# A 32-head attention with a gated MLP on one core: the first tiles of x and V's weights in another order, and a unit's shift by one-tensor steps

## The chip, the core and the metric

The kernel runs on one core of a Trainium2 chip. The metric is the device time of one execution in microseconds. The kernel before takes 1639.81 us, the median of three runs (1638.86 to 1640.61).

## The reference

x is 2048 x 512, in float32. There are 32 heads of 16 elements; the MLP has 1792 hidden elements.

```python
xn = _layernorm(x, axis=-1)
qkv = (xn @ wqkv).reshape(B, S, 3, H, Dh)            # q, k, v
scores = einsum("bhqd,bhkd->bhqk", q, k) * Dh ** -0.5
s = (softmax(scores) @ v).reshape(B, S, D) @ wo
h = xn @ w1 + b1
g = silu(square(max(h, 0)) @ w2 + b2)
return x + s * g
```

## The kernel before, in words

Every product is made in float32 from three reduced products: each operand is split into a high and a low part, and high x high, high x low and low x high are added up (`terms3`). A split is two instructions, one that rounds to the high part and one that subtracts it (L82 and L83 on GpSimd; with `hi_act` the first is on ScalarE).

**The ramp** (loop at L1146 to L1172) brings 16 tiles of x through the layernorm: statistics on VectorE (`ln_stats`), the normalized tile on ScalarE (`ln_norm`, L1089), four transposes on TensorE and the high part on ScalarE (`ln_high`, L1096 and L1098), the low part on VectorE (`ln_low`, L1104). V's weights (`wa_t`, four pieces of 128 rows called ko 0 to 3) are split on GpSimd ahead of the loop (L1144). Between the transposes, `pump(n)` puts n matmuls of a waiting tile of Q, K or V on TensorE (L991); such a full-array tile has 12 matmuls. Each engine works through its own list in the order in which the program is written.

**The lead loop** (L1212 to L1260) makes the rest of Q, K and V in half-array pieces, 24 matmuls to a tile (`lead_halves`, L1040). Beside them run the first max matmuls (L305) with their reductions (L313): for each query row, the largest score over 512 keys is taken.

**The main loop** has 512 slots. 16 slots make a unit, a quad of heads with a quarter of the queries. A slot has four score matmuls (L1283), four exponentials (L1289), four groups of products with V (L379, here called PV), and between them max matmuls for later units and the matmuls of the MLP (L239, L207) and of the output product (L787), which are called dense work. `long_slots` (L1365) handles two slots at a time in one of two forms. The form of *seven* has seven max matmuls and runs the PV groups of two slots together, 16 matmuls in a row. The form of *eight* has eight max matmuls and two separate runs of 8. Whether a pair of slots takes the form of seven is decided by `ahead_m`: only if enough maxima have been made for the units to come. `hosts` picks the slots in which a unit's shift falls.

**The shift of a unit** (`shift`, L336 to L365) follows the unit's last max reduction by two slots (`late`, L332). It reduces 64 partial maxima to 16 (L338), makes the high and the low part of the negated maximum (L340 and L343, two instructions that read two tensors each; L340 reads a tile of zeros) and transposes them (L347). Then `keep` writes them to HBM (`sh_d`, L350) one slot later, and `back` reads them as two more rows of the score matmul's operand (`qe`, L370). Unit u needs these rows at slot 16u. `later(n, fn)` puts such a step on a waiting list that is worked off n slots later, in the order of the list; the DMAs themselves go through one queue, SyncE's, in that same order. On it stand, near the end, also `wo_small` (L675, four small loads of the tile h, L682), the output product's operand (`oc`, L701), the tiles g and xr of the output (L726, L731), the stores of the finished heads (`on_d`, L426) and the loads of q for the max matmuls (`qm`, L135 and L140).

**The output** of a tile (`post`, L770 to L782) multiplies the product with g on VectorE (L780) and adds x on GpSimd.

Of the kernel before, what the change touches and what calls it, by code (L numbers as in the profile page):

```python
# [8 lines left out]
F32 = mybir.dt.float32  # L9
F32R = mybir.dt.float32r  # L10
# [6 lines left out]
P = 128  # L17
# [23 lines left out]
def kernel(  # L41
# [28 lines left out]
    make_identity(nc, ident)  # L70
    eps_t = const.tile([P, 1], F32, name="eps_t")
    nc.vector.memset(eps_t, EPS)
    zero = const.tile([P, 16], F32, name="zero")
    nc.vector.memset(zero, 0.0)
    b1_t = const.tile([P, FO], F32, name="b1_t")
    b2_t = const.tile([P, D], F32, name="b2_t")

# [20 lines left out]
    with ExitStack() as ph:  # L98
# [84 lines left out]
        waiting = []  # L183
        now = [0]

        def later(n, fn):
            waiting.append((now[0] + n, fn))

        def run_waiting(all_=False):
            due = [w for w in waiting if all_ or w[0] <= now[0]]  # L190
# [138 lines left out]
                if s == 15:  # L329
                    late.append((now[0] + 2, u))  # L330

        def shift_due():  # L332
            if late and late[0][0] <= now[0]:
                shift(late.pop(0)[1])

        def shift(u):  # L336
            m4 = sp.tile([P, 16], F32, name="m4")
            nc.vector.tensor_reduce(m4, mxs[u], axis=AX.X, op=ALU.max)  # L338
            sh = sp.tile([P, 2, 16], F32R, name="sh")
            nc.vector.scalar_tensor_tensor(  # L340
                sh[:, 0], m4, -1.0, zero, op0=ALU.mult, op1=ALU.add
            )
            nc.vector.scalar_tensor_tensor(  # L343
                sh[:, 1], m4, -1.0, sh[:, 0].bitcast(F32), op0=ALU.mult, op1=ALU.subtract
            )
            sq = sp.tile([P, 32], F32, name="sq")
            nc.vector.transpose(sq, sh.rearrange("p i c -> p (i c)").bitcast(F32))  # L347

            def keep():
                nc.sync.dma_start(sh_d[u].rearrange("r (b q) -> b r q", q=32), sq)  # L350

            def back():
                for p in range(2):
                    for i in range(2):
                        shift_rows(u, p, i)

            if in_loop:
                later(1, keep)
                later(max(2, 16 * u - 9 - now[0]), back)
            else:  # L360
                keep()
                if u < 2:
                    back()
                else:
                    waiting.append((16 * u - 9, back))  # L365
# [371 lines left out]
        def wo_part():  # L737
            for k in range(15):
                c, tt = WO_ORDER[k]
                if k == 0:  # L740
                    later(2, lambda: wo_load(3))
                if k == 2:
                    later(2, lambda: wo_load_last(3))
                if k == 5:
                    wo_load(0)
                if k == 6:
                    later(2, lambda: wo_load_last(0))
                if k == 9:
# [12 lines left out]
                g, xr = wos.pop(k)  # L761
                wide = c < 2 and m_free()
                if wide and "w" not in free_ps:
                    free_ps["w"] = [pm.tile([P, 512], F32, name="pm_t") for _ in range(3)]
                ps = [pd.tile([P, D], F32, name="pd_t")]
                ps.append(free_ps["w"][2] if wide else ps[0])
                if c > 1:
                    s = tail[c, tt] = tail["p"].tile([P, D], F32, name=f"ts{c}{tt}")

                def post():  # L770
                    if c > 1:
                        nc.scalar.activation(s, ps[0], AF.Copy)
                        nc.gpsimd.tensor_tensor(s, s, g, op=ALU.mult)
                        nc.gpsimd.tensor_tensor(s, s, xr, op=ALU.add)
                        return
                    if wide:
                        h = wos["f"].tile([P, D], F32, name="h", bufs=2)
                        nc.vector.tensor_tensor(h, ps[1], g, op=ALU.mult)
                        nc.gpsimd.tensor_tensor(xr, xr, h, op=ALU.add)
                    nc.vector.tensor_tensor(g, ps[0], g, op=ALU.mult)  # L780
                    nc.gpsimd.tensor_tensor(g, g, xr, op=ALU.add)
                    later(2, lambda g=g, t0=t0: nc.sync.dma_start(of[t0 : t0 + P, :], g))  # L782

                def emit(lane, n, i, m, kos):
                    r = slice(64 * lane, 64 * lane + 64)
                    a, b = ((0, 0), (0, 1), (1, 0))[i]
                    inst = nc.tensor.matmul(  # L787
                        ps[lane], oc[r, a, n, ts_], wot[r, b, n],
                        start=m == 0 and (lane == 0 or wide), stop=m == kos and (lane == 1 or wide),
                        skip_group_check=True,  # L790
                    )
                    if m == 0 and last_use[0] is not None and not wide:
                        tc.add_manual_dep(
                            inst.ins, last_use[0].ins.name,
                            mybir.DependencyInfo(
                                mybir.DependencyClass.Sync, mybir.DependencyReason.DATA
                            ),
                            reason="the other row tile is done with the bank",
                        )

                units = []
                for lane in range(2):
                    kos = [0, 1, 2] + [3] * (c < 2 or lane == 0)
                    terms = [(n, i) for n in kos for i in range(3)]
# [336 lines left out]
            load_x(t)  # L1141
        for vt in vts:
            nc.vector.memset(vt[:, :, DH:], 1.0)
        for ko in range(KO):  # L1144
            split((wa_t[:, 0, ko, 2 * P :], wa_t[:, 1, ko, 2 * P :]), raw_v[:, ko])
        for i in range(NT + 3):  # L1146
            if i == 1:
                ln_norm(0)
            if i < NT:
                ln_stats(i)  # L1150
            if 0 < i - 1 < NT:
                ln_norm(i - 1)
            if 0 <= i - 3 < NT:
                ln_low(i - 3)
            if 0 <= i - 2 < NT:
                ln_high(i - 2)
            if i in (3, 4):
                kos = slice(2 * i - 6, 2 * i - 4)
                split((wa_t[:, 0, kos, : 2 * P], wa_t[:, 1, kos, : 2 * P]), raw_m[:, kos])
            if 6 <= i < 10:  # L1160
                fill_ring("ka", i // 2 - 3, 1.0, (32 + 64 * (i % 2),))
            if i in (10, 11):
                fill_ring("qm", i - 10, 0.0)
            if i == 11:
                raw_r = [load_w("wv", 3 * P, ((P, 3 * P),))]
            if i >= 3:
                rest.append(("v", (i - 3) % 4, (i - 3) // 4))
                if i % 4 == 2:
                    c = (i - 3) // 4
                    ahead.append(("qk", 4, c))  # L1170
                    (rest if c else ahead).append(("qk", 0, c))
                pump(8 if i > 3 else 6)  # L1172
        while ahead:
            pump(1)
        lx.close()
# [131 lines left out]
        def dense():  # L1307
# [3 lines left out]
            wo_pools()  # L1311
            wo_ask(0)
            wo_ask(1)
            later(3, wo_small)
            yield from wo_part()

        pts = {}
# [37 lines left out]
                n + 4 * max(0, 16 * u - SHIFT - st) >= 64 * (u + 1) for u in range(n // 64, NU)  # L1355
            )

        host = [0]

        def hosts(st):  # L1360
            if late and st > host[0] + 4:
                host[0] = st + 2
            return st <= host[0]

        def long_slots(st0, units, post, wide=False):  # L1365

# [25 lines left out]
            for h in range(2):  # L1392
# [4 lines left out]
                if wide:  # L1397
# [9 lines left out]
                    shift_due()  # L1407
                    for kb in (st - 2, st - 1):
                        pv_step(kb, pts.pop(kb))
                elif n == 12 and ahead_m(  # L1410
                    sum(done_m) + 7 - (0 if hosts(st) else max(0, 450 - st) // 16 * 2), st + 2
                ):
                    visit(h, "s" + "D" * n + "s", ".mmsmssmsmssmm")
                    begin(st + 1)
                    max_end()
# [3 lines left out]
                else:  # L1419
# [2 lines left out]
                    else:  # L1422
                        visit(h, "D" * n + ".", "msmsmsmsms")
                    max_end()
                    shift_due()
                    pv_step(st - 2, pts.pop(st - 2))
                    begin(st + 1)
                    if n == 12:
# [1 line left out]
                    else:  # L1430
                        visit(h, "ss..", "mmsm", True)
                    max_end()
                    shift_due()
                    pv_step(st - 1, pts.pop(st - 1))
            if post is not None:
                last_use[0] = None
# [90 lines left out]
```

## Time and profile before

| | |
|---|---|
| median of three runs | 1639.81 us |
| the profiled execution | 1642.99 us |
| its span in the profile | 1641.1 us |
| TensorE busy | 1621.3 us |
| VectorE busy | 1350.6 us |
| ScalarE busy | 1181.7 us |
| GpSimd busy | 516.4 us |

The span runs from the first to the last instruction in the trace; the profiled execution's own time has 1.9 us more around it, and lies 3.2 us above the median of the runs. Rows of a timeline give the start, the duration, the engine, the line, the operation, what it writes and reads, and in brackets how long its engine had been idle before and what ended that. SPq is SyncE's queue; its rows are DMA issues, not transfers. In the chain of waits, a row gives the start, the duration and the engine of one piece of the chain that ended last.

### The profile page before, as it was taken

How to read it: one execution, taken by the hardware profiler on the slowest of the kernel's cores; microseconds unless marked ns; L12 is line 12 of the kernel's file. 1: busy time of each engine (PE TensorE's matmuls, PEld its weight loads, DVE VectorE, ACT ScalarE, POOL GpSimd, SP SyncE). 2: the span in 40 equal slices, each digit the busy share in tenths (PEclk: the TensorE clock that was granted, in tenths of full speed). 3: DMA queues.
4: the chain of work that ended last, by engine and by line, in shares of the span. 5: the costliest groups of instructions: out<-in, count | busy, mean ns of one | idle time of the engine just before them, and what ended most of it. 6: DMA issues, size and time to landing. Idle time of an engine off the chain costs nothing.

```text
span 1641.1 us, 35386 instructions
## 1 busy us (share of the span) xinstructions
PE 1621.3 (99%) x13627; PEld 979.2 (60%) x13627; DVE 1350.6 (82%) x2335; ACT 1181.7 (72%) x2339; POOL 516.4 (31%) x541
## 2 busy tenths in 40 slices
PE   7999999999999999999999999999999999999998
PEld 6799666556656655565566556645665565454455
DVE  6399988887788888888888888888888888888843
ACT  6221477778878877787777777877877777777785
POOL 5335567513211321222123103311331133213224
PEclk9899999999999999999999999999999999999999
DMA  8596555426232522342333423343341442415444
GB/s 304 158 270 222 180 177 163 130 54 170 86 87 83 162 72 81 102 128 70 93 99 111 114 71 111 95 107 82 112 121 50 105 142 62 105 48 171 122 147 143
DMA packets 150465, 201.44 MB, mean 123 GB/s; under 512 B 50008, under 2 KB 67416, under 8 KB 148760
## 3 DMA queue, kind: packets, MB, share of 16 engines
q1 hardware_dynamic: 150296, 199.17, 41.6%
q8 instruction: 108, 1.77, 0.5%
q14 instruction: 61, 0.50, 0.1%
HBM read 144.84 MB, written 53.99 MB: 121 GB/s over the span
## 4 chain that ended last, share of the span: by engine, by line
PE 94%; DVE 2%; issue 2%; DMA 1%; POOL 0%; SPq 0%; ACT 0%; DVEq 0%
PE po L379 30%; PE pm_t L305 17%; PE pd_t L239 17%; PE se L1283 15%; PE pd_t L207 5%; PE se L1040 3%; PE pd_t L787 2%; DVE mx L313 2%; PE pd_t L1040 1%; PE po L1040 1%; PE se L991 1%; DMA ka<-k_d 1%; PE pm_t L1283 0%; DMA xt<-in_A_x_dram 0%; POOL wr_t L944 0%
## 5 line engine op out<-in xcount | busy, mean ns | idle before, releaser
L313 DVE TENSOR_REDUCE mx<-pm_t 128x1 f32<-128x512 f32 x2048 | 1267.9, 683 | 208.7 <-PE pm_t L305 123.1
L1289 ACT ACTIVATE pt<-se 128x512 f32<-128x512 f32 x1738 | 924.0, 615 | 227.3 <-PE se L1283 156.5
L305 PE MATMUL pm_t<-ka,qm 64*128 64x512 f32 x2048 | 784.5, 418 | 4.2 <-DVE mx L313 2.4
L1283 PE MATMUL se<-qe,ka 64*128 64x512 f32 x2009 | 735.0, 413 | 0.4 <-DMA qe<-sh_d 0.2
L379 PE MATMUL po<-pt,v 128*32 128x512 f32 x3554 | 526.6, 602 | 0.0
L305 PEld LDWEIGHTS pm_t<-ka,qm 64*128 64x128 f32 x2048 | 360.6, 185 | 219.5 <-DVE mx L313 205.2
L1283 PEld LDWEIGHTS se<-qe,ka 64*128 64x128 f32 x2009 | 350.5, 184 | 103.1 <-ACT pt L1289 61.8
L239 PEld LDWEIGHTS pd_t<-xc,w1s 64*128 64x128 f32 x2352 | 295.7, 187 | 47.3 <-issue 45.3
L239 PE MATMUL pd_t<-xc,w1s 64*128 64x256 f32 x2352 | 322.0, 286 | 0.0
L239 PE MATMUL pd_t<-w2t,hT 64*128 64x512 f32 x936 | 253.2, 406 | 0.0
L379 PE MATMUL po<-ex,v 128*32 128x512 f32 x542 | 226.5, 602 | 0.0
L1289 ACT ACTIVATE ex<-se 128x512 f32<-128x512 f32 x271 | 163.4, 616 | 42.1 <-PE se L1283 30.2
L239 PEld LDWEIGHTS pd_t<-w2t,hT 64*128 64x128 f32 x936 | 159.5, 184 | 48.5 <-issue 40.2
L379 PEld LDWEIGHTS po<-pt,v 128*32 128x32 f32 x3554 | 88.2, 108 | 154.3 <-issue 141.1
L558 POOL TENSOR_TENSOR r<-r 128x512 f32<-128x512 f32 x49 | 50.9, 1039 | 331.9 <-ACT r L555 331.9
L577 POOL TENSOR_TENSOR u<-u,b_t 128x512 f32<-128x512 f32 x16 | 20.7, 1296 | 365.0 <-ACT u L576 365.0
L207 PE MATMUL pd_t<-w2t,hT 64*128 64x512 f32 x408 | 106.1, 392 | 0.0
L207 PEld LDWEIGHTS pd_t<-w2t,hT 64*128 64x128 f32 x408 | 72.5, 184 | 9.6 <-DVE mx L313 0.7
L787 PE MATMUL pd_t<-wot,oc 64*128 64x512 f32 x267 | 76.9, 406 | 0.0
L417 POOL TENSOR_TENSOR ot<-ot,hl 128x512 f32<-128x512 f32 x31 | 39.8, 1284 | 109.1 <-DMA hl<-r_d 80.9
L83 POOL TENSOR_TENSOR hT<-r,hT 128x512 fp32r<-128x512 f32 x56 | 72.2, 1289 | 4.7
L1040 PE MATMUL se<-xT,wr_t 64*128 64x512 f32 x336 | 71.4, 390 | 0.0
(133 smaller groups left out, 1213.4 us busy)
## 6 DMA issues: line engine op xcount, KB each, us to landing
w1s<-w_d SPq DMA_DIRECT2D x196, 256.0 KB
k_d<-hl SPq DMA_DIRECT2D x32, 256.0 KB
xn_d<-xT SPq DMA_DIRECT2D x8, 1024.0 KB
q_d<-hl SPq DMA_DIRECT2D x16, 512.0 KB
qm<-q_d SPq DMA_DIRECT2D x128, 64.0 KB
qe<-q_d SPq DMA_DIRECT2D x128, 64.0 KB
ka<-k_d SPq DMA_DIRECT2D x32, 256.0 KB
hl<-r_d SPq DMA_DIRECT2D x31, 256.0 KB
```

The costliest lines, as they stand in the source:

```text
L83: (lo or nc.gpsimd).tensor_tensor(dst[1], raw, dst[0].bitcast(F32), op=ALU.subtract)
L207: mm = nc.tensor.matmul(out_, lh(r), rh(r), start=first_ and lane == 0, stop=last_ and lane == 1, skip_group_check=True,)
L239: mm = nc.tensor.matmul(out_, lh(r), rh(r), start=first_ and lane == 0, stop=last_ and lane == 1, skip_group_check=True,)
L305: nc.tensor.matmul(ps, qms[u][p][64 * j : 64 * j + 64, qb * P : (qb + 1) * P], kas[qd, p][64 * j : 64 * j + 64, kc * 512 : (kc + 1) * 512] ...
L313: return nc.vector.tensor_reduce(mxs[u][:, c, kc : kc + 1], ps, axis=AX.X, op=ALU.max)
L379: nc.tensor.matmul(po[32 * j : 32 * j + 32, :], vs[qd][:, (4 * kb + j) * VW : (4 * kb + j) * VW + 32], pts[j], start=(kb == 0), stop=(kb = ...
L417: nc.gpsimd.tensor_tensor(ot, ot, hl[:, 1].bitcast(F32), op=ALU.mult)
L558: nc.gpsimd.tensor_tensor(r, r, r, op=ALU.mult)
L787: inst = nc.tensor.matmul(ps[lane], oc[r, a, n, ts_], wot[r, b, n], start=m == 0 and (lane == 0 or wide), stop=m == kos and (lane == 1 or ...
L1040: inst = nc.tensor.matmul(out_, lh(r), rh(r), start=first_ and lane == 0, stop=last_ and lane == 1, skip_group_check=True,)
L1283: nc.tensor.matmul(se, kas[qd, j // 2][b : b + 64, kb * P : (kb + 1) * P], qes[u][j // 2][b : b + 64, :], start=True, stop=True,)
L1289: return nc.scalar.activation(pts[j], se, AF.Exp, scale=0.25)
```

## The change

Five things are changed.

1. `shift` is written as three reductions that read one tensor each: the maximum, the negated maximum (the high part), and the negated sum of these two (the low part). The tile of zeros goes.
2. `keep` and `back` go to the front of the waiting list. In the form of eight a shift may come two slots later than before (`shift_due(2)`).
3. The form of seven is taken for couples of pairs, that is for four slots at once, with another rule on how many maxima are kept in hand (`seven` in place of `hosts`).
4. In the output's `post` the product is copied by ScalarE and multiplied with g by GpSimd while max matmuls are still to be made and the tile isn't a wide one. `wo_small` comes 8 slots after the asking rather than 3.
5. In the ramp the high parts of ko 2 and 3 of V's weights are made on ScalarE. The first tile's transposes come one step of the loop earlier, and the first V tile is started behind one tile of x rather than two.

```diff
-        def later(n, fn):
-            waiting.append((now[0] + n, fn))
+        def later(n, fn, first=False):
+            waiting.insert(0 if first else len(waiting), (now[0] + n, fn))
...
-        def shift_due():
-            if late and late[0][0] <= now[0]:
+        def shift_due(slack=0):
+            if late and late[0][0] + slack <= now[0]:
                 shift(late.pop(0)[1])
...
-            m4 = sp.tile([P, 16], F32, name="m4")
-            nc.vector.tensor_reduce(m4, mxs[u], axis=AX.X, op=ALU.max)
-            sh = sp.tile([P, 2, 16], F32R, name="sh")
-            nc.vector.scalar_tensor_tensor(
-                sh[:, 0], m4, -1.0, zero, op0=ALU.mult, op1=ALU.add
-            )
-            nc.vector.scalar_tensor_tensor(
-                sh[:, 1], m4, -1.0, sh[:, 0].bitcast(F32), op0=ALU.mult, op1=ALU.subtract
-            )
+            sh = sp.tile([P, 3, 16], F32R, name="sh")
+            nc.vector.tensor_reduce(sh[:, 0].bitcast(F32), mxs[u], axis=AX.X, op=ALU.max)
+            nc.vector.tensor_reduce(sh[:, 1], mxs[u], axis=AX.X, op=ALU.max, negate=True)
+            with nc.allow_low_precision(reason="the low part of a sum of two, exact in float32"):
+                nc.vector.tensor_reduce(
+                    sh[:, 2], sh[:, :2].bitcast(F32).rearrange("p i c -> p c i"),
+                    axis=AX.X, op=ALU.add, negate=True,
+                )
...
-                later(1, keep)
-                later(max(2, 16 * u - 9 - now[0]), back)
+                later(1, keep, True)
+                later(max(2, 16 * u - 9 - now[0]), back, True)
...
-                    nc.vector.tensor_tensor(g, ps[0], g, op=ALU.mult)
+                    else:
+                        h = ps[0]
+                        if not m_free():
+                            h = wos["f"].tile([P, D], F32, name="h", bufs=2)
+                            nc.scalar.activation(h, ps[0], AF.Copy)
+                    (nc.vector if wide or m_free() else nc.gpsimd).tensor_tensor(
+                        g, ps[0] if wide else h, g, op=ALU.mult
+                    )
...
-        for ko in range(KO):
-            split((wa_t[:, 0, ko, 2 * P :], wa_t[:, 1, ko, 2 * P :]), raw_v[:, ko])
+        def split_v(ko, hi_act):
+            split(
+                (wa_t[:, 0, ko, 2 * P :], wa_t[:, 1, ko, 2 * P :]), raw_v[:, ko], hi_act=hi_act
+            )
+
+        for ko in range(2):
+            split_v(ko, False)
         for i in range(NT + 3):
+            if 2 <= i < 4:
+                if i == 2:
+                    ln_high(0)
+                ln_norm(i - 1)
+                if i == 3:
+                    ln_high(1)
+                split_v(i, True)
+                ln_low(i - 2)
+                rest.append(("v", i - 2, 0))
...
-                pump(8 if i > 3 else 6)
+            if i >= 2:
+                pump(8 if i > 3 else 9 - 3 * (i - 2))
...
-            later(3, wo_small)
+            later(8, wo_small)
...
-        host = [0]
-
-        def hosts(st):
-            if late and st > host[0] + 4:
-                host[0] = st + 2
-            return st <= host[0]
+        couple = [False]
+
+        def seven(st):
+            if couple[0]:
+                couple[0] = False
+                return True
+            kept = 0 if late and st % 4 == 2 else max(0, 450 - st) // 16 * 2
+            couple[0] = ahead_m(sum(done_m) + 14 - kept, st + 4)
+            return couple[0]
...
-                elif n == 12 and ahead_m(
-                    sum(done_m) + 7 - (0 if hosts(st) else max(0, 450 - st) // 16 * 2), st + 2
-                ):
+                elif n == 12 and seven(st):
...
-                    shift_due()
+                    shift_due(2)
```

Three places in the order of the instructions follow. The first is TensorE's list at the start of the ramp (`pm_t` from `ident` and `xn` are the transposes of a tile of x, `se` the matmuls of Q, K and V). Before:

```order
L1096 MATMUL pm_t<-ident,xn 128x128 x8
L991 MATMUL se<-wa_t,xT_189 128x512 x6
L1096 MATMUL pm_t<-ident,xn 128x128 x4
L991 MATMUL se<-wa_t,xT_189 128x512 x8
L1096 MATMUL pm_t<-ident,xn 128x128 x4
L991 MATMUL se<-wa_t,xT_189 128x512 x8
L1096 MATMUL pm_t<-ident,xn 128x128 x4
L991 MATMUL se<-wa_t,xT_189 128x512 x2
```

And now:

```order
L1100 MATMUL pm_t<-ident,xn 128x128 x4
L995 MATMUL se<-wa_t,xT_187 128x512 x9
L1100 MATMUL pm_t<-ident,xn 128x128 x4
L995 MATMUL se<-wa_t,xT_187 128x512 x6
L1100 MATMUL pm_t<-ident,xn 128x128 x4
L995 MATMUL se<-wa_t,xT_187 128x512 x8
L1100 MATMUL pm_t<-ident,xn 128x128 x4
L995 MATMUL se<-wa_t,xT_187 128x512 x8
```

Nine matmuls of the first V tile now stand between the transposes of the first and of the second tile of x, and six between the second and the third.

The second place is ScalarE's list at the same stage (`xn` is a normalized tile of x, `xT` the high part of its transpose, `vt` a finished tile of V). Before:

```order
L1080 ACTIVATE rstd<-mv,eps_t 128x1
L1089 ACTIVATE xn<-xt,rstd 128x512
L1080 ACTIVATE rstd<-mv,eps_t 128x1 x2
L1089 ACTIVATE xn<-xt,rstd 128x512
L1098 ACTIVATE xT_189<-pm_t 128x4x128
L1080 ACTIVATE rstd<-mv,eps_t 128x1
L1089 ACTIVATE xn<-xt,rstd 128x512
L1098 ACTIVATE xT_189<-pm_t 128x4x128
L1080 ACTIVATE rstd<-mv,eps_t 128x1
L1089 ACTIVATE xn<-xt,rstd 128x512
L1098 ACTIVATE xT_189<-pm_t 128x4x128
L1000 ACTIVATE vt_192<-se 128x32x16
```

And now:

```order
L1084 ACTIVATE rstd<-mv,eps_t 128x1
L1093 ACTIVATE xn<-xt,rstd 128x512
L1084 ACTIVATE rstd<-mv,eps_t 128x1
L1102 ACTIVATE xT_187<-pm_t 128x4x128
L1093 ACTIVATE xn<-xt,rstd 128x512
L78 ACTIVATE wa_t<-wv 128x512
L1084 ACTIVATE rstd<-mv,eps_t 128x1
L1093 ACTIVATE xn<-xt,rstd 128x512
L1102 ACTIVATE xT_187<-pm_t 128x4x128
L78 ACTIVATE wa_t<-wv 128x512
L1084 ACTIVATE rstd<-mv,eps_t 128x1
L1004 ACTIVATE vt_190<-se 128x32x16
```

The two rows that write `wa_t` are new, and the second of them stands behind the second tile's `xT`.

The third place is SyncE's queue near the end of the program, around the shift of unit 29 (`sh_d_94` is that shift in HBM; `hl` are finished heads). Before:

```order
L411 DMA hl<-r_d_124 128x1x512
L682 DMA h<-in_A_wo_dram 16x512 x4
L701 DMA oc_21211<-on_d_129 128x2x512
L701 DMA oc_21211<-on_d_130 128x2x512
L701 DMA oc_21211<-on_d_131 128x2x512
L726 DMA g<-g_d 128x512
L731 DMA xr<-in_A_x_dram 128x512
L586 DMA g_d<-u 128x512
L350 DMA sh_d_94<-sq 4x32x32
L426 DMA on_d_132<-hl 16x2x512 x4
L370 DMA qe_736<-sh_d_94 2x512 x2
L370 DMA qe_737<-sh_d_94 2x512 x2
```

And now:

```order
L583 DMA g_d<-u 128x512
L423 DMA on_d_132<-hl 16x2x512 x4
L133 DMA qm_201<-q_d_60 32x512
L138 DMA qm_201<-q_d_60 16x512
L133 DMA qm_201<-q_d_60 32x512
L138 DMA qm_201<-q_d_60 16x512
L347 DMA sh_d_94<-sq 4x32x32
L679 DMA h<-in_A_wo_dram 16x512 x4
L723 DMA g<-g_d 128x512
L728 DMA xr<-in_A_x_dram 128x512
L367 DMA qe_749<-sh_d_94 2x512 x2
L367 DMA qe_750<-sh_d_94 2x512 x2
```

The write of the shift (`sh_d_94<-sq`) stood ahead of the stores of `on_d` and stands now behind them and behind four loads of `qm`. The load of `h`, a tile of g and one of xr have come between the write and the reads of its rows (`qe<-sh_d_94`).

More of the change, by code (lines that the diff above doesn't have):

```diff
@@ L72 @@
     nc.vector.memset(eps_t, EPS)
-    zero = const.tile([P, 16], F32, name="zero")
-    nc.vector.memset(zero, 0.0)
     b1_t = const.tile([P, FO], F32, name="b1_t")
@@ L330, in max_end @@
                     late.append((now[0] + 2, u))
-        def shift_due():
-            if late and late[0][0] <= now[0]:
+        def shift_due(slack=0):
+            if late and late[0][0] + slack <= now[0]:
                 shift(late.pop(0)[1])
         def shift(u):
-            m4 = sp.tile([P, 16], F32, name="m4")
-            nc.vector.tensor_reduce(m4, mxs[u], axis=AX.X, op=ALU.max)
-            sh = sp.tile([P, 2, 16], F32R, name="sh")
-            nc.vector.scalar_tensor_tensor(
-                sh[:, 0], m4, -1.0, zero, op0=ALU.mult, op1=ALU.add
-            )
-            nc.vector.scalar_tensor_tensor(
-                sh[:, 1], m4, -1.0, sh[:, 0].bitcast(F32), op0=ALU.mult, op1=ALU.subtract
-            )
+            sh = sp.tile([P, 3, 16], F32R, name="sh")
[6 more added lines that the diff above has]
+                )
             sq = sp.tile([P, 32], F32, name="sq")
-            nc.vector.transpose(sq, sh.rearrange("p i c -> p (i c)").bitcast(F32))
+            nc.vector.transpose(sq, sh[:, 1:].rearrange("p i c -> p (i c)").bitcast(F32))
             def keep():
@@ L1150 @@
                 ln_stats(i)
-            if 0 < i - 1 < NT:
+            if 4 <= i < NT + 1:
                 ln_norm(i - 1)
-            if 0 <= i - 3 < NT:
+            if 5 <= i:
                 ln_low(i - 3)
-            if 0 <= i - 2 < NT:
+            if 4 <= i < NT + 2:
                 ln_high(i - 2)
@@ L1165 @@
                 raw_r = [load_w("wv", 3 * P, ((P, 3 * P),))]
-            if i >= 3:
+            if i >= 5:
                 rest.append(("v", (i - 3) % 4, (i - 3) // 4))
@@ L1432, in long_slots @@
                     max_end()
-                    shift_due()
+                    shift_due(2)
                     pv_step(st - 1, pts.pop(st - 1))
```

## The prediction

> **What bounds the kernel now.** I read the page first: the busy share of each engine and the chain of work that ended last, by engine.
>
> ```profile
> PE 1621.3 (99%) x13627; PEld 979.2 (60%) x13627; DVE 1350.6 (82%) x2335; ACT 1181.7 (72%) x2339; POOL 516.4 (31%) x541
> PE 94%; DVE 2%; issue 2%; DMA 1%; POOL 0%; SPq 0%; ACT 0%; DVEq 0%
> ```
>
> TensorE is busy 99% of the span and holds 94% of the chain. Time can be won only where TensorE waits, where it is given less work, or where its clock is low. Next the chain in order of time, for the length of a step of the main loop.
>
> ```profile
> 451.02 1.85 PE po L379 x16
> 456.48 1.85 PE po L379 x16
> ...
> 1191.00 1.00 PE po L379 x8
> 1196.70 1.00 PE po L379 x8
> ```
>
> A pair of slots in the form of seven takes 456.48 - 451.02 = 5.46 us, one in the form of eight 1196.70 - 1191.00 = 5.70 us. Changing one seven into an eight costs 0.24 us; the eight makes one maximum more.
>
> Third, the granted clock by stretches of 3.41 us (columns: stretch, length, PE busy and count, granted clock, DMA share, GB/s), the last of those at 0.50 ending at 78.24, and what stood on TensorE in the fourth of them.
>
> ```profile
> 6.56:9.97 3.41, 1.51 (x9) 1.00 1.00 346
> 9.97:13.38 3.41, 3.41 (x13) 1.00 1.08 367
> 23.62:27.03 3.41, 2.81 (x15) 1.00 1.02 375
> 64.58:68.00 3.42, 2.50 (x13) 1.00 1.03 184
> 68.00:71.41 3.41, 3.41 (x13) 0.50 0.93 304
> ...
> 78.24:81.65 3.41, 3.41 (x32) 1.00 0.16 57
> ...
> 66.36 0.47 PE L305 MATMUL pm_t<-ka,qm 64*128 64x512 f32 x1 [0.92 <-DMA ka<-k_d]
> ```
>
> After a wait of 0.92 us the clock is at one half for 10.24 us, three such stretches, which costs 5.1 us of work. An idle time of 0.60 us in a stretch (23.62) has no such effect. So in this trace a wait of TensorE of about a microsecond or more costs more than itself. The Trainium skill, "TensorE: Matmul & The Clock Gate", has the clock fall only after a window of some 3.4 us without work and come back after as long a busy one; the row at 64.58 disagrees, since TensorE was busy 73% of that stretch. By the page the price of such a drop would be 1.7 us, as an estimate.
>
> **The change, part by part.**
>
> *The shift.* Its four instructions, in all 32 units (min/median/max ns), and one case on VectorE, on GpSimd, and PV on TensorE:
>
> ```profile
> L338 DVE TENSOR_REDUCE m<-mx x32: 207/209/220, 119.2 to 1569.7; 128x16 f32<-128x64 f32 x32
> L340 DVE SCALAR_TENSOR_TENSOR sh<-m,zero x32: 174/175/961, 119.4 to 1570.0; 128x16 fp32r<-128x16 f32 x32
> L343 DVE SCALAR_TENSOR_TENSOR sh<-m,sh x32: 174/174/1218, 119.7 to 1570.5; 128x16 fp32r<-128x16 f32 x32
> ...
> 207.65 0.96 DVE L340 SCALAR_TENSOR_TENSOR sh<-m,zero 128x16 fp32r<-128x16 f32 x1
> ...
> 207.54 1.04 POOL L516 TENSOR_TENSOR r<-r 128x512 f32<-128x512 f32 x1 [3.12 <-ACT r L513]
> ...
> 203.47 1.07 PE L379 MATMUL po<-pt,v 128*32 128x512 f32 x8
> 206.35 1.07 PE L379 MATMUL po<-pt,v 128*32 128x512 f32 x8
> 210.11 1.06 PE L379 MATMUL po<-pt,v 128*32 128x512 f32 x8
> ```
>
> L340 ended at 208.61, just as GpSimd's 1.04 us did (208.58). L338, which reads one tensor, never took over 220 ns. So an instruction that reads two tensors waits for GpSimd, one that reads one doesn't; the Trainium skill, "SBUF — State Buffer", "SBUF: two separate sides", tells of such a lock of a shared port. In this case PV came 3.76 us after the one before it instead of 2.88: 0.88 us on the path. L340 and L343 have one such case more each that I count at the same price or somewhat over it, the longest by 1218 - 174 ns = 1.04 us. Three cases, less the 0.2 us that an undisturbed shift adds: **-2.5 us** (-3.1 to -1.5). Two instructions of 174 ns become two reductions, of 207 ns by L338 for the long one and no more for the short: 0.07 us in each of 32 units, most of it under TensorE's work: +0.1 (0 to 2.2).
>
> *Seven and eight.* By the rules of the two programs there are 74 pairs of seven before and 69 after, 113 and 118 of eight, and 170 maxima are made ahead of the main loop instead of 165. Five pairs cost 5 x 0.24 = **+1.2**. Sevens that come right behind an eight with the MLP's closing step fall from 9 to 4; what such a step can have cost is bounded by TensorE's whole wait for maxima in the run:
>
> ```profile
> L305 PE MATMUL pm_t<-ka,qm 64*128 64x512 f32 x2048 | 784.5, 418 | 4.2 <-DVE mx L313 2.4
> ```
>
> 2.4 us in all; a fifth of it, **-0.5** (-1.4 to 0).
>
> *The output's product.* VectorE's multiplication:
>
> ```profile
> L780 DVE TENSOR_TENSOR g<-pd_t,g x8: 682/691/692, 1556.7 to 1621.2; 128x512 f32<-128x512 f32 x8
> ```
>
> Only those move that come while max matmuls are still to be made. They free 0.69 us of VectorE in a step each; ScalarE (72%) and GpSimd (31%) take it up. A 0.69 us that fits between the reductions costs nothing today: **-0.3** (-0.7 to 0).
>
> *The lead loop.* One tile of 24 half-array matmuls becomes one of 12 on the full array.
>
> ```profile
> 80.00:170.00 90.00, 89.52 (x640) 1.00 0.73 234
> ...
> 50.39 5.76 PE L991 MATMUL se<-wa_t,xT 128*128 128x512 f32 x24
> ```
>
> L1040 alone has 640 matmuls in 90 us, so 24 take 3.38 us, with the maxima beside them; 24 on the full array take 5.6 us from start to start (50.39 to 55.98), so 12 take 2.8. **-0.6**.
>
> *The ramp.*
>
> ```profile
> 6.18 1.09 PE L1096 MATMUL pm_t<-ident,xn 128*128 128x128 f32 x4 [6.18 <-POOL wa_t L83]
> ...
> 9.94 2.91 PE L991 MATMUL se<-wa_t,xT 128*128 128x512 f32 x6
> 13.35 2.12 PE L991 MATMUL se<-wa_t,xT 128*128 128x512 f32 x8
> ...
> 15.47 0.44 PE pm_t L1096 x4
> ...
> 11.03 1.29 POOL L83 TENSOR_TENSOR wa_t<-wv,wa_t 128x512 fp32r<-128x512 f32 x1
> ...
> 9.02 0.58 ACT L1098 ACTIVATE xT<-pm_t 128x512 fp32r<-128x512 f32 x1
> ...
> 25.28 0.66 PE L1096 MATMUL pm_t<-ident,xn 128*128 128x128 f32 x4 [0.60 <-ACT xn L1089]
> 30.40 0.50 PE L991 MATMUL se<-xT,wa_t 128*128 128x512 f32 x1 [0.56 <-DVE xT L1104]
> ```
>
> The first transposes start at 6.18 and their place doesn't move. With 0.6 us for xT, the first V matmul can start near 8 instead of 9.94. The first nine run at 0.43 us each (2.91 us for six, at the cold start) to 11.9, the second tile's transposes to 13.0, its xT on ScalarE to 13.6, the high part of ko 3 behind it to 14.2, GpSimd's low part (1.29) to 15.5. Only then can the eleventh matmul run, and the first V tile is done at 16.0. By then the program before has issued 14 matmuls of V and four transposes, the new one 12 and two: two matmuls and two transposes behind, 2 x 0.23 + 2 x 0.44 = 1.4 us. Two later waits, 0.60 and 0.56 us, are for ScalarE and VectorE and shrink by what TensorE is late: -1.2. **+0.2** (-1.2 to +1.5), and 1.7 us of idle time in 13.38 to 16.79, whose clock is the first rival below.
>
> *The rows of unit 29.* In the tail there are only eights, and with the slack of two its shift comes at slot 459 instead of 457, two slots or 5.7 us later; the rows are needed at slot 464 both times.
>
> ```profile
> 1484.52 1.81 SPq L682 DMA_DIRECT2D h<-in_A_wo_dram  x4
> ...
> 1491.12 0.56 SPq L350 DMA_DIRECT2D sh_d<-sq  x1
> 1493.26 2.12 SPq L426 DMA_DIRECT2D on_d<-hl  x4
> 1497.42 2.02 SPq L370 DMA_DIRECT2D qe<-sh_d  x4
> 1499.54 0.34 SPq L135 DMA_DIRECT2D qm<-q_d  x1
> ...
> 1501.32 1.56 SPq L726 DMA_DIRECT2D g<-g_d  x1
> ...
> 1500.07 0.47 PE L1283 MATMUL se<-qe,ka 64*128 64x512 f32 x1 [0.22 <-DMA qe<-sh_d]
> ```
>
> Already TensorE waits 0.22 us for these rows, 2.65 us after their first issue (1497.42 to 1500.07). Now `sq` is ready near 1496.8. The stores of on_d, which wait for GpSimd, end at 1495.4 as before, four loads of qm take 1.8 (1499.54 to 1501.32) to 1497.2; then the write of the shift, 0.56, the loads of h, 1.81, g and xr, 0.9: the rows are asked for at 1500.5, and TensorE has them at 1500.5 + 2.65 = 1503.1 instead of 1500.07. **+3.1** (0, if the queue runs ahead, to +6, if the write lands as late as in this trace, some 6 us after its issue). A wait of over 3 us must leave more than 0.92 us in a stretch, so by the row at 64.58 the clock halves for 10.24 us: 5.1 us, less what of it falls into the wait itself; I take **+3.6** (0 to 5.1). TensorE's own list stands still behind the score matmul, and with it all exponentials and maxima.
>
> Sum: -2.5 + 0.1 + 1.2 - 0.5 - 0.3 - 0.6 + 0.2 + 3.1 + 3.6 = +4.3. The profiled execution (1642.99, span 1641.1) is 3.2 above the median; the difference is put on the median: 1639.8 + 4.3 = **1644.1 us**.
>
> **The rivals.**
> 1. *Slower still: the clock falls in the ramp too.* The 1.7 us of idle time in 13.38 to 16.79 is more than the 0.92 at 64.58. For it speaks that row; against it, that at the start one busy stretch (9.97 to 13.38) brought full speed, whatever the 1.9 us of idle time before. +1.7 for one stretch, +5.1 for three: 1645.8 to 1649.2, say 1649. It decides from about 0.9 us idle in one stretch.
> 2. *Not slower: unit 29's rows come in time.* For it: the three large loads of oc, behind which the write of the shift landed late in this trace, are over earlier now, since the loads of h no longer stand ahead of them. Against it: even a write that lands at once leaves the reads behind the issues counted above. It decides if these issues end 3 us sooner. Then 3.1 and 3.6 go: 1637.4.
> 3. *Not slower: the clock doesn't fall at 68.* The wait of 0.92 us for ka moves with the ramp; if the ramp is 1.6 to 2.6 us late, it falls on the border of two stretches, some 0.5 us in each, under the 0.6 that had no effect: -5.1, 1639.0, and with rival 2, 1632.3.
> 4. *The change doesn't do what it says:* the reductions wait for GpSimd as well, three of them instead of two instructions. L338's 220 ns speaks against it. The 2.5 us stay and half as much comes on top: 1647.9.
>
> **How the numbers follow.** Forecast 0.40, rival 1 0.15, rival 2 0.23, rival 3 0.17, rival 4 0.05. A measurement of this kernel tells 0.2% (3.3 us) from no change: below 1636.5 is faster, above 1643.1 slower. The forecast (1641 to 1647 with its own bounds) lies above for three quarters, rivals 1 and 4 wholly: 0.48 slower. Faster are a part of rivals 2 and 3, where the bounds of the shift and of the ramp (to -1.2) help or both come together: 0.25. The same: 0.27. The range, 1634.5 to 1649.5, takes in rivals 1 and 4 and most of 2 and 3.
>
> **What would show it.** The sharpest sign: at slot 464, near 1500 us, an exponential's score matmul that waits some 3 us for qe<-sh_d, and a granted clock of 0.50 in the three stretches behind it. No wait over 0.5 us there, and the main term is wrong. The longest of the three reductions should stay under 250 ns, and PV near 207 us should keep its 2.9 us. The first V tile should be finished near 16 us; a clock of 0.50 between 17 and 27 us is rival 1, one of 1.00 between 68 and 78 us rival 3. The forecast is wrong by its kind if the loop's steps themselves, 5.46 and 5.70 us, change.

## The result, and the profile after

The changed kernel takes 1643.95 us, the median of 16 runs (1642.80 to 1651.67); the kernel before takes 1639.45 us on the same chips (16 runs, 1638.30 to 1640.90). The ratio is 1.0033, with a 95% interval of 1.0024 to 1.0042: 4.5 us slower. The profiled execution of the changed kernel took 1643.80 us and is a typical one. That of the kernel before (1642.99 us) is not: all 16 of those runs were faster. This matters below.

On the page of the changed kernel, the busy times by engine, the chain by engine, and two groups of matmuls (busy time, mean ns | idle time ahead of them and what ended it):

```profile
PE 1619.0 (99%) x13615; PEld 978.3 (60%) x13615; DVE 1344.4 (82%) x2332; ACT 1184.1 (72%) x2343; POOL 517.4 (32%) x541
PE 95%; DMA 1%; DVE 1%; SPq 1%; issue 1%; ACT 0%; POOL 0%; DVEq 0%; POOLq 0%
L303 PE MATMUL pm_t<-ka,qm 64*128 64x512 f32 x2048 | 786.1, 417 | 2.0 <-DVE mx L311 0.9
L1302 PE MATMUL se<-qe,ka 64*128 64x512 f32 x2009 | 731.8, 412 | 4.3 <-DMA qe<-sh_d 4.3
```

The group of score matmuls says it already: 4.3 us of idle time, all of it behind one DMA, `qe<-sh_d`; before, 0.2 us were. The timeline of TensorE has the place, and that of SyncE's queue what came ahead of it:

```profile
1494.35 1.06 PE L376 MATMUL po<-pt,v 128*32 128x512 f32 x8
...
1500.16 0.76 PE L1302 MATMUL se<-qe,ka 64*128 64x512 f32 x1 [4.31 <-DMA qe<-sh_d]
...
1489.87 1.74 SPq L423 DMA_DIRECT2D on_d<-hl  x4
1491.71 0.37 SPq L133 DMA_DIRECT2D qm<-q_d  x1
...
1493.68 0.56 SPq L347 DMA_DIRECT2D sh_d<-sq  x1
1494.34 1.81 SPq L679 DMA_DIRECT2D h<-in_A_wo_dram  x4
1496.19 0.42 SPq L723 DMA_DIRECT2D g<-g_d  x1
1496.65 0.43 SPq L728 DMA_DIRECT2D xr<-in_A_x_dram  x1
1497.18 2.01 SPq L367 DMA_DIRECT2D qe<-sh_d  x4
```

One more row of VectorE, and one of the queue's own waits between 1478 and 1500 us (total, times, longest):

```profile
1484.45 0.21 DVE L344 STREAM_TRANSPOSE sq<-sh 128x32 f32<-128x32 f32 x1
...
SPq L423 <- POOL hl L416: 5.4, 1, 5.4
```

The shift itself is ready at 1484.45 + 0.21 = 1484.66, and its write is issued at 1493.68. It isn't late on VectorE: for 9 us it sits in the program's order behind the stores of `on_d`, for which SyncE waits 5.4 us until GpSimd has made `hl`, and behind four loads of `qm`.

Then the clock, by stretches (length, PE busy and count, granted clock):

```profile
13.38:16.80 3.42, 1.65 (x5) 0.94 1.05 405
16.80:20.21 3.41, 3.41 (x12) 0.56 0.57 155
...
64.58:68.00 3.42, 3.42 (x16) 1.00 1.16 331
68.00:71.41 3.41, 3.41 (x15) 1.00 0.95 163
...
1494.89:1498.30 3.41, 0.96 (x10) 0.92 0.47 118
1498.30:1501.71 3.41, 1.55 (x8) 0.50 0.50 147
1501.71:1505.13 3.42, 3.42 (x22) 0.58 0.63 171
1505.13:1508.54 3.41, 3.41 (x28) 1.00 0.00 1
```

The clock falls twice, near 16.5 and near 1498 us, and there is no low clock at 68. The second low clock lasts from about 1497.8 to 1504.6 (0.92 and 0.58 are means of 1.00 and 0.50). Only its part from 1500.16 on falls on work: 4.4 us at half speed, a loss of 2.2 us. The ramp shows two waits for V's weights:

```profile
8.07 4.18 PE L995 MATMUL se<-wa_t,xT 128*128 128x512 f32 x9 [0.92 <-ACT xT L1102]
12.05 1.05 PE L1100 MATMUL pm_t<-ident,xn 128*128 128x128 f32 x4
14.31 0.50 PE L995 MATMUL se<-wa_t,xT 128*128 128x512 f32 x1 [1.21 <-ACT wa_t L78]
15.65 1.90 PE L995 MATMUL se<-wa_t,xT 128*128 128x512 f32 x5 [0.85 <-POOL wa_t L81]
17.35 1.06 PE L1100 MATMUL pm_t<-ident,xn 128*128 128x128 f32 x4
```

And the shift by reductions, over all 32 units (min/median/max ns):

```profile
L336 DVE TENSOR_REDUCE sh<-mx x32: 207/210/220, 121.2 to 1569.4; 128x16 f32<-128x64 f32 x32
L337 DVE TENSOR_REDUCE sh<-mx x32: 208/210/215, 121.3 to 1569.5; 128x16 fp32r<-128x64 f32 x32
L339 DVE TENSOR_REDUCE sh<-sh x32: 186/188/191, 121.6 to 1569.8; 128x16 fp32r<-128x32 f32 x32
```

None is over 220 ns.

### The profile page after: what moved, and what is told of

Its sections match the earlier page's. It is cut to its first block, busy times and chain, and to the rows that moved or that the text cites. A ratio compares the mean times of both kernels' runs of the same rounds, so it can differ in the third digit from the quotient of the medians.

```text
span 1642.0 us, 35371 instructions
## 1 busy us (share of the span) xinstructions
PE 1619.0 (99%) x13615; PEld 978.3 (60%) x13615; DVE 1344.4 (82%) x2332; ACT 1184.1 (72%) x2343; POOL 517.4 (32%) x541
## 4 chain that ended last, share of the span: by engine, by line
PE 95%; DMA 1%; DVE 1%; SPq 1%; issue 1%; ACT 0%; POOL 0%; DVEq 0%; POOLq 0%
PE po L376 30%; PE pd_t L237 17%; PE pm_t L303 17%; PE se L1302 15%; PE pd_t L205 6%; PE se L1044 3%; PE se L995 2%; PE pd_t L791 2%; PE pd_t L1044 1%; PE po L1044 1%; DVE mx L311 1%; DMA g_d<-u 1%; DMA xr<-in_A_x_dram 0%; PE pm_t L1302 0%; PE pm_t L1100 0%
```

## The experiments

Each kernel was timed in turn with the kernel before on the same chip. Times are medians, ratios are to the kernel before, which took 1639.26 to 1639.65 us there. Where two profiles are set against each other, the measure is the time at which a PV group ends in the one and in the other; the n-th group is that of the n-th slot.

### Which of the two kernels' profiles is typical

Of 30 runs of the kernel before, taken beside a_slack0, b_slack2, b_shift and b_ramp, 27 took 1637.6 to 1640.4 us, with a mean granted clock of 0.999 or 1.0, and three took 1644.5 to 1645.0 at 0.996 or 0.997. A clock of one half for 10.24 us of a span of 1641 lowers the mean by 0.003. Beside the other kernels it was four of 31 runs and none of 11. So, as far as these means tell, the low clock behind the wait for `ka`, on which the prediction's rule was built, comes in about one run of ten. The profile of b_slack2 below, whose program is the kernel before up to unit 29's shift, hasn't got it:

```profile
64.58:68.00 3.42, 3.42 (x18) 1.00 0.99 185
68.00:71.41 3.41, 3.13 (x14) 1.00 1.00 337
```

Its main loop begins 3.7 us earlier than in the profile of before. It is the yardstick in what follows up to slot 456. It is one execution: in the five profiles with the ramp of before and no low clock at 68, the first PV group ends between 188.7 and 189.7 us (189.5 here), so a start of the main loop is known to about half a microsecond.

### The wait for unit 29's rows

**a_slack0**: the changed kernel without the slack near the end.

```diff
-                    shift_due(2)
+                    shift_due(2 if st < 448 else 0)
```

> The changed kernel, but without the slack of two slots from slot 448 on, so that unit 29's shift comes at slot 457 as before. Theory (the wait for unit 29's rows and the low clock behind it cost the changed kernel 4.1 + 2.1 us): TensorE waits under 0.6 us at slot 464, the clock stays at 1.00 there, and the time falls by 6 us to about 1637.8 (ratio to before 0.999). Rival (the wait only took the place of waits that other steps of the tail would have had): under 2 us won, 1642 or more.

Measured: 1637.32 us, ratio 0.9986 (0.9977 to 0.9994); 6.6 us less than the changed kernel, and faster than the kernel before. The write of the shift now stands ahead of `on_d`:

```profile
1483.29 0.56 SPq L347 DMA_DIRECT2D sh_d<-sq  x1
1483.89 0.80 SPq L583 DMA_DIRECT2D g_d<-u  x1
1492.48 2.01 SPq L367 DMA_DIRECT2D qe<-sh_d  x4
1494.60 1.74 SPq L423 DMA_DIRECT2D on_d<-hl  x4
```

TensorE has no wait for these rows any more and the clock stays at 1.00. Wait and low clock together cost the whole loss and 2 us more.

**b_slack2**: the kernel before, with the slack from slot 448 to 461 alone.

```diff
-                    shift_due()
+                    shift_due(2 if 448 <= st < 462 else 0)
```

> The kernel before with one thing changed: the slack of two slots in the form of eight from slot 448 to 461, so unit 29's shift moves from slot 457 to 459. Theory: the write of the shift now stands behind the stores of on_d and four loads of qm; its rows come some 2 us sooner than in the changed kernel, since the loads of h don't stand between: a wait of 2 to 2.5 us at slot 464, the clock halved behind it, +4 us (1643.5). Rival (the loads of h and the front place in the waiting list make the wait): under 0.6 us of wait, no change.

Measured: 1643.82 us, ratio 1.0025 (1.0013 to 1.0037). The size of the loss is as expected; a change of one number in one step of the kernel before gives about the same loss as the whole change. Its profiled execution, at 1639.98 us, is one of the two fastest of its 12 runs and shows only part of it:

```profile
1492.50 0.56 SPq L350 DMA_DIRECT2D sh_d<-sq  x1
1494.48 2.02 SPq L370 DMA_DIRECT2D qe<-sh_d  x4
...
1497.09 0.47 PE L1283 MATMUL se<-qe,ka 64*128 64x512 f32 x1 [1.02 <-DMA qe<-sh_d]
```

The rows are asked for 2.7 us sooner than in the changed kernel, and TensorE waits 1.0 us, less than expected, without a low clock behind it. Nine of its 12 runs have a mean clock of 0.998 or less. That longer waits with a low clock behind them make the other 4 us is read from these means and shown by no profile.

**a_small3**: the changed kernel with the loads of h asked for after 3 slots.

```diff
-            later(8, wo_small)
+            later(3, wo_small)
```

> The changed kernel with the four loads of h asked for 3 slots after the start as before, not 8, so that they leave the queue between the write of unit 29's shift and the reads of its rows. Theory (each issue between them counts): the rows are asked for 1.8 us earlier, the wait of 4.3 us falls to 2.5, the time by 1.8 to 2.7 us (1641.7). Rival (the write's landing decides): the wait stays over 4 us, no change.

Measured: 1640.14 us, ratio 1.0003 (0.9991 to 1.0014): 3.8 us less than the changed kernel, more than expected. Its profiled execution is the slowest of its 12 runs (1646.32 us): behind 2.0 us of idle time ahead of the first max matmul, at 73.27 us, the clock is at one half for 13.7 us. One stretch of these, and the place at unit 29's rows:

```profile
74.82:78.24 3.42, 3.42 (x12) 0.50 0.95 286
...
1501.52 2.03 SPq L367 DMA_DIRECT2D qe<-sh_d  x4
...
1504.31 0.47 PE L1302 MATMUL se<-qe,ka 64*128 64x512 f32 x1 [2.35 <-DMA qe<-sh_d]
```

The wait for the rows is 2.35 us instead of 4.31, and the clock stays at 1.00 behind it. Against a_slack0, 2.8 us are lost from slot 456 to 464, and 6.5 in the changed kernel. So each issue between the write and the reads counts. That a shorter wait is also less often followed by a low clock is what this one profile and the means suggest (five of 12 runs at 0.997 or less, in the changed kernel 12 of 16); it isn't shown. The deferral of `wo_small`, made by the change itself, put four loads into the one place where they did harm.

### The shift by reductions

**b_shift**: the kernel before with the three reductions alone (the diff's part on `shift`).

> The kernel before with the shift by three reductions of one tensor alone. Theory: -2.5 us (1637.0), the three steps near 207, 255 and 1107 us without their extra 0.8 to 1.1 us, no reduction over 250 ns. Rival (reductions wait for GpSimd as well): some reduction takes over 500 ns, no gain or a loss of up to 2 us.

Measured: 1635.67 us, ratio 0.9973 (0.9963 to 0.9983): 3.6 us faster. Against the yardstick, 0.87 us are gained at PV group 7, 0.84 by group 23 and 1.09 by group 328, the three units named in advance, and up to group 456 no more than 0.2 us beside. In the changed kernel it looks like this on TensorE, at the place where one PV group came 3.76 us after the other before:

```profile
201.87 1.06 PE L376 MATMUL po<-pt,v 128*32 128x512 f32 x8
204.74 1.06 PE L376 MATMUL po<-pt,v 128*32 128x512 f32 x8
207.63 1.07 PE L376 MATMUL po<-pt,v 128*32 128x512 f32 x8
210.53 1.06 PE L376 MATMUL po<-pt,v 128*32 128x512 f32 x8
213.59 1.07 PE L376 MATMUL po<-pt,v 128*32 128x512 f32 x8
```

The step in which the shift runs (207.63 to 210.53) takes 2.9 us, and the one behind it 0.2 more.

### The ramp

**b_ramp**: the kernel before with the new ramp alone.

> The kernel before with the new ramp alone. Theory: the ramp ends some 2 us later for the half clock and the waits for V's weights near 13 to 20 us, and one tile more on the full array saves 0.6 us: +1 to +2 us if the low clock at 68 us of the profile of before is there in neither or in both, and -3 if the new ramp does away with it. Rival (the ramp is hidden behind the wait for ka at 65 us): within 0.5 us of before.

Measured: 1646.18 us, ratio 1.0042 (1.0027 to 1.0057), a loss of 6.9 us, which neither theory gave. Its profile (1649.85 us, slower than five of the other six runs) has a low clock of 10 us near 75 us, and waits for `qe<-sh_d` of 1.9 and 0.3 us near 1505, so only part of the 6.9 us is the ramp itself. In that profile the first PV group ends 6.8 us behind the yardstick, of which the low clock of 10.24 us is 5.1; 0.5 more are lost up to slot 456. Against the profile of before, another 2.0 us are lost at unit 29's rows and 1.6 between slots 481 and 489. With this ramp 165 maxima are made ahead instead of 170, fewer pairs take the form of seven (69 up to slot 487, against 74), and the later shifts move. How the median's 6.9 us split up wasn't separated.

**a_slack0_oldramp**: a_slack0 with the ramp of before.

> The kernel of a_slack0 with the ramp of the kernel before. Theory (the new ramp is a loss: the main loop of the changed kernel starts some 2 us later than in a run of the old ramp without a low clock at 68 us): 2 us faster than a_slack0, 1635.3. Rival (the new ramp is a gain, or hidden): 1637 or more.

Measured: 1637.17 us, ratio 0.9986 (0.9973 to 0.9999); 0.2 us from a_slack0, so the rival holds on the whole. In the profiles two things work against each other. The main loop begins 2.6 us earlier than in a_slack0, and up to slot 456 the lead grows to 4.7 us. Then 6.2 us are lost, 2.0 up to PV group 489 and 4.2 at group 495. With the old ramp 170 maxima are made ahead instead of 165, the couples fall otherwise, and the last unit's shift is done behind PV group 489 instead of 486; TensorE waits for its rows, with a low clock of 3.4 us behind the wait:

```profile
1580.54 0.46 PE L1287 MATMUL se<-qe,ka 64*128 64x512 f32 x1 [2.28 <-DMA qe<-sh_d]
```

Its 12 runs spread from 1634.70 to 1643.42.

**a_slack0_mend**: a_slack0 with one step moved on ScalarE.

```diff
-                if i == 3:
-                    ln_high(1)
-                split_v(i, True)
+                if i == 2:
+                    split_v(2, True)
+                    split_v(3, True)
+                if i == 3:
+                    ln_high(1)
```

> The kernel of a_slack0 with one thing moved in the ramp: the high part of V's fourth piece of weights (ko 3) stands on ScalarE right behind that of ko 2, ahead of the second tile's xT. Theory (that piece, behind xT of the second tile and GpSimd's low part behind it, holds TensorE up by 2 us near 13 to 15.6 us): both waits of 1.2 and 0.9 us for wa_t go, the second tile of x is done 1 to 2 us earlier, and the whole by 1 to 2 us (1636). Rival (the ramp's end is set by the wait for a normalized tile near 36 us and for the keys behind it): the waits go, the time stays within 0.5 us of a_slack0.

Measured: 1633.60 us, ratio 0.9964 (0.9951 to 0.9978), the fastest kernel here: 3.7 us less than a_slack0. The waits for `wa_t` are gone, and so is the low clock behind them:

```profile
7.89 4.18 PE L995 MATMUL se<-wa_t,xT 128*128 128x512 f32 x9 [0.78 <-ACT xT L1102]
11.87 1.03 PE L1100 MATMUL pm_t<-ident,xn 128*128 128x128 f32 x4
12.58 2.23 PE L995 MATMUL se<-wa_t,xT 128*128 128x512 f32 x6
14.64 0.60 PE L1100 MATMUL pm_t<-ident,xn 128*128 128x128 f32 x4
15.00 2.11 PE L995 MATMUL se<-wa_t,xT 128*128 128x512 f32 x8
...
13.38:16.80 3.42, 3.42 (x16) 1.00 1.05 405
```

The third tile's transposes start at 14.64 instead of 17.33, and the main loop 3.0 us earlier than in a_slack0; the gap is 3.3 us at the end. The two waits of a_slack0 (1.21 and 0.86 us) and 1.7 us for 3.41 us at half clock would be 3.8 us together; they went with one and the same edit, so the runs don't tell their shares apart.

### The couples and the output's product

**b_couples**: the kernel before with `seven` in place of `hosts` alone.

> The kernel before with the form of seven chosen for couples of pairs alone. Theory (the choice only moves a few steps of 0.24 us): within 1 us of before. Rival (the couples cost or bring several microseconds through where the shifts fall): 2 us or more either way.

Measured: 1644.18 us, ratio 1.0026 (1.0015 to 1.0037). The rival was right: a loss of 4.5 us, though the program has 75 pairs of seven up to slot 487 against 74. Against the yardstick, 0.5 us go between slots 140 and 200, 0.6 between 320 and 360, 1.6 to slot 400 and 1.2 to slot 440. Against the profile of before, 1.3 go between slots 481 and 489, where the last unit's shift is done behind PV group 490 instead of 486. By the program's rule (`seven` drops the maxima kept in hand only while a shift is pending) I took the missing slack for the cause.

**b_couples_slack**: b_couples with the slack up to slot 448.

> The kernel of b_couples with the slack of two slots in the form of eight, up to slot 448 only. Theory (the couples alone lose since 10 units' shifts then fall into an eight, where VectorE has no room; with the slack they fall into the couple): the 4 us that b_couples lost over before come back, within 1 us of before or better, down to -2.5. Rival (the couples themselves lose, wherever the shift falls): 1643 or more.

Measured: 1643.87 us, ratio 1.0037 (1.0024 to 1.0049), on 6 runs. The time didn't come back. The theory falls for the time as a whole. In its profile (1641.52 us, its fastest run) the main loop loses 1.6 us from slot 140 to slot 400 instead of 2.8, but the loss behind slot 480, here 2.0 us with the last shift behind PV group 490 again, is there. What the rest of its runs lose stays open. The couples are no gain by themselves on the kernel before; in the changed kernel they stand on 165 maxima, and the last shift is done behind PV group 486.

**a_mend_oldpost**: a_slack0_mend with VectorE's multiplication.

```diff
-                    (nc.vector if wide or m_free() else nc.gpsimd).tensor_tensor(
-                        g, ps[0] if wide else h, g, op=ALU.mult
-                    )
+                    nc.vector.tensor_tensor(g, ps[0], g, op=ALU.mult)
```

> The kernel of a_slack0_mend with the output's product multiplied by g on VectorE again. Theory (the profile's 1.0 us between slot 463 and the end is this edit's): 1 us slower than a_slack0_mend, 1634.6, all of it behind slot 474. Rival (the move is hidden): no difference, within 0.3 us.

Measured: 1633.96 us, ratio 0.9969 (0.9958 to 0.9981), 0.36 us more than a_slack0_mend. Between the two theories, and too little for six and eight runs to show by their medians alone: in the profiles 0.35 us are lost between slots 474 and 484 and nothing else changes behind 440. The other 0.6 us of that stretch are not this edit's.

## Why the prediction was right, and where it wasn't

The forecast was +4.3 us; +4.5 was measured, and the largest term, the rows of unit 29, is the one that was named. That the sum came within 0.2 us is luck: the ramp was forecast 2.5 us too low, and gains in the tail of about 1.6 us that no step had, with 0.6 more from the shift, made up for it. By its steps, measured against a run of before without a low clock at 68:

| step | predicted, us | measured, us |
|---|---|---|
| unit 29's rows, with the clock behind them | +3.1 + 3.6 = +6.7 | +6.6 (changed kernel less a_slack0) |
| the shift by reductions | -2.5 + 0.1 | -3.0 (b_shift, first slot to slot 456) |
| pairs of seven and eight | +1.2 - 0.5 | +0.8 (a remainder: changed kernel, first slot to 456: -2.2, less the shift's -3.0) |
| ramp and lead loop | +0.2 - 0.6 | +2.05 (first PV group) |
| the output's product | -0.3 | -0.35 (a_mend_oldpost) |
| other parts of the tail | none | about -1.6 (a remainder: 4.5 less the rows above) |

*Unit 29's rows.* The size of the sum was right, its split less so: 4.1 us more waiting rather than 3.1, and 2.2 to 2.5 of low clock rather than 3.6. The clock fell 1.9 us into the wait and for two stretches, not behind it for three, so that 2.4 of its 6.8 us cost nothing. The prediction named two grounds for the write's late issue: `sq` ready only near 1496.8, and the queue. The first was wrong: `sq` was ready at 1484.66, 9 us ahead of its issue. The prediction added the two slots to the issue of the write before (1491.12), as if that had waited for its data; this row of the kernel before shows that the data was ready at 1483.04:

```profile
1482.83 0.21 DVE L347 STREAM_TRANSPOSE sq<-sh 128x32 f32<-128x32 f32 x1
```

The second ground, the order behind on_d and qm, was the whole of it, and the rival that the rows come in time failed on the 5.4 us that SyncE stood waiting for GpSimd.

*The ramp.* This is the step that failed; it was mis-sized: with the lead loop -0.4 was forecast and +2.05 measured. The chain from xT of the second tile to the high and the low part of ko 3 was walked right (14.2 and 15.5 against 14.31 and 15.65 measured), and so was the idle time in 13.38 to 16.80. Two things behind it were not.

First, the 1.2 us that later waits were to give back were not given back. TensorE's waits from 20 us to the end of the full-array work are 1.78 us in the changed kernel, 1.07 of them at 35.84 for a normalized tile, against 1.15 in b_slack2. In a_slack0_mend, where TensorE comes there 2.9 us earlier than in a_slack0, that wait is 1.05 us against 1.06: it doesn't shrink by what TensorE is late.

Second, the first rival, a low clock in the ramp, came true for one stretch and not for three (0.56 in 16.80 to 20.21); 3.41 us at one half are 1.7 us of work. At the transposes of the fifth tile the changed kernel is 3.0 us behind b_slack2 (23.10 less 2.1 for nine matmuls more, against 17.99), where 1.4 were forecast; at the end of the full-array work it is 3.5 behind (71.20 less 2.8 for twelve matmuls more, against 64.93). The lead loop then gives back 1.4, more than the 0.6 forecast. What the low clock costs from run to run is uncertain: three of 11 runs of a_slack0 have a mean clock of 1.0 instead of 0.998 or 0.999 and are not faster (1637.84 to 1638.19).

*The clock at 68.* The rule taken from one row, "0.92 us of wait, then 10.24 us at half", is no rule. b_shift waited 1.0 us for `ka` and kept its clock:

```profile
64.58:68.00 3.42, 2.39 (x12) 1.00 1.00 185
68.00:71.41 3.41, 3.35 (x18) 1.00 0.97 320
```

b_ramp idled 1.9 us in one stretch near 1503 at 1.00. The Trainium skill, "TensorE: Matmul & The Clock Gate" ("What's actually happening"), says that the window in which TensorE's activity is watched is free-running and doesn't start with the kernel. By that the same wait could fall otherwise into it from run to run, which would fit three runs of 30 for one and the same program; that this is the cause here, no run shows. The Trainium skill's rule in the same section, that the clock falls after at least one idle window of some 3.4 us, is at odds with the row of before at 64.58, where TensorE was busy 2.50 of 3.42 us. The third rival, which lived on the low clock at 68 going away, was without object, since a typical run of before hasn't got it. For the same reason it was right to put the difference on the median and not on the profiled execution, whose own 1642.99 us lay only 0.8 us below the changed kernel's 1643.80. Nor does the new ramp rule such a low clock out: in b_ramp and a_small3 it comes at 74 and 73 us, behind 0.9 and 2.0 us of idle time.

*The shift.* Right in cause, place and nearly in size. The fourth rival is out: of the 96 reductions of the changed kernel 40 ran at the same time as a GpSimd operation, and none took over 220 ns.

*The tail.* About 1.6 us were won behind slot 456 that no step had; the prediction's list stopped at the product. In the profiles, 0.7 us of it lie at PV groups 461 to 463, where a_slack0 has none of the kernel before's wait of 0.22 us for unit 29's rows, and 0.6 between groups 483 and 487. There the changed kernel takes a pair in the form of seven (groups 485 and 486 in one run of 16 matmuls), though the prediction had only eights in the tail. That this form is the cause wasn't tried alone, and the rest stays open.

## What to carry to other kernels

A transfer that is late need not be so because its data is late: read, on the queue that issues it, which instruction ahead of it waits, and for how long. A change that moves a step by two slots is priced by what it is moved behind; here a good edit (reductions that read one tensor, 3.6 us) was hidden under one number in another (the slack near the end, 6.6 us) and one place in ScalarE's order (3.7 us). And look at the spread of the runs before a profile is taken as the kernel: what one execution shows may be what one in ten does.

## What of the hardware was not expected

In programs that are alike up to there, a wait of 0.92 us for `ka` was followed by 10.24 us at a clock of one half (before), and one of 1.0 us by none (b_shift). A low clock lasted 3.4 us (ramp), 6.8 us (behind unit 29's rows), 10.2 us (before, from 68) or 13.7 us (a_small3, from 73), in the last two with TensorE busy almost all the time. An instruction of 0.17 us on VectorE that reads two tensors took up to 1.22 us beside a GpSimd operation, while the reductions of 0.19 to 0.21 us that replaced it never took more than 0.22.
